# A gated mix of a long convolution and a GELU layer on one core: new front schedule, bias seeded in PSUM, output pairs read back in the loop

## The chip, the core and the metric

One core of a Trainium2 chip. TensorE (PE) multiplies, VectorE (DVE) and ScalarE (ACT) do elementwise work, GpSimd (POOL) and SyncE (SP) issue transfers here, ACT a few; DMA engines move the data between memory and the core. SBUF is the working memory, PSUM the eight banks (128 partitions of 512 fp32 each) into which TensorE writes. The metric is the time of one execution in microseconds (us), as a median over runs; less is better.

## The reference

The input x has 2048 rows (time) and 512 columns (channels). Everything is fp32.

```python
x = A_u                                             # (1, 2048, 512)
g = sigmoid((x * gate_w).sum(-1, keepdims=True))    # one gate per row
# a: per channel d a causal convolution over time with K[d, l], plus a skip term
K = einsum("dn,dnl,dn->dl", Cc, exp(dt * A * l), dt * Bc).real     # 128 complex modes n
a = irfft(rfft(pad(x)) * rfft(pad(K)))[:2048] + x * Dskip
# b: a two-layer network, 512 -> 1792 -> 512
b = gelu(x @ w1 + b1) @ w2 + b2
out = g * a + (1 - g) * b
```

## The kernel before

The kernel has three parts: a *front*, a *loop* of 16 steps and a *last stage*. The convolution is done as a transform in two stages, a product per frequency, and the inverse in two stages.

**Front** (`front`, lines 317 to 1070). Four streams of tasks share the engines:

- `dense`: the network b. Each fp32 factor is split into a rounded part and a remainder ("h" and "l"), and a product is made of three matmuls. The hidden layer has 14 columns of 128. Time is cut into 8 blocks of 256 rows, and the 8 blocks are run twice, once for each half of the hidden columns, so there are 16 passes (b = 0 to 15) of four steps each: 64 steps. A step does `hidden` (L889, matmuls L899 to L901, gelu L916, rounding L919, remainder L929) for one or two columns, and `output` (L933, matmuls L947 to L949), which adds into one of two PSUM accumulators `acc`, one for each 128 rows of the block. After the fourth step ACT scales an accumulator by 1 - g into `io` (L968) and it is stored to `out` (first half, plain, SP) or added to it in memory (second half, an accumulating transfer on POOL). In the first half, before a pass's first product, a matmul of a matrix of ones with a two-row tile (rounded b2 and its remainder) starts the accumulation with the bias (L942); `bias` (L848) prepares that tile.
- `signal`: 8 tasks, each the first transform stage of 256 rows of x. Two tiles `ux` are loaded (L417), `first_stage` (L392) makes 16 matmuls (L403) into four PSUM banks, ACT copies the four banks to tiles of a ring `st` of three (L421), and SP stores each tile in two halves to memory, `tu_d` (L424).
- `taps`: makes K. DVE and ACT build powers, magnitudes and phases for 16 groups of 32 channels, `contract` (L671) multiplies them out on PE (L681, 128 matmuls a group), and for each two groups `first_stage` runs on the result; the tables are stored to `tk_d` (L723).
- `early`: loads 27 of the 32 tiles of `tu_d` back into SBUF (L446), into places that other work has left.

The order in which the front's tasks stand on each engine is not written by hand. Each task has an engine, a modelled length and a due time; `Plan.run` (L231) walks a clock, gives every engine the earliest due task whose inputs are ready by its model, and the instructions are emitted in that order. The constants at the top set the due times: `T_0` and `T_MLP` for the dense steps, `K_0` and `T_KG` for the taps, `U_0` and `U_GAP` for the signal, `W_*` for curves laid over them, and `D_*` for offsets of single tasks (`D_EV` for the copies out of the first stage's banks and the scaling L968, `D_S1` for the first stage's matmuls, `D_XL` for the loads of x). Each queue is in order: an instruction that waits holds up all that stand behind it on its engine, SP's transfers included.

**Loop** (`conv`, L1073). For each of 16 steps: `signal(s + 1)` (8 matmuls, second stage of the signal, four banks with the tag `pu`), `taps(s + 2)` (8 matmuls, ACT copies the result, L1116), `product(s)` (six DVE operations), `inverse(s)` (8 matmuls, L1147, two banks with the tag `pa`) and `turn(s)`: ACT copies to `sa` (L1153), SP stores to `t4_d` (L1155), and after each fourth step four transfers of 512 KB bring a group back across partitions into `den` and `t3` (L1163; on POOL, for the last group on ACT). The loads of the tap tables for later steps (L1089) are on SP too. Some products of the network's last pass (`late`) run on PE at the end of the loop.

**Last stage** (L1230). Eight pairs of output tiles, m = 0 to 7: eight matmuls (L1236) into two banks; for m < 6 DVE scales one bank by g and ACT the other (L1248, L1250), and POOL adds the pair to `out` in memory with an accumulating store (L1255). Pairs 6 and 7 were loaded from `out` in loop steps 12 and 13 (L1220); DVE does their scaled add (L1246) and plain stores follow (L1252, L1257).

Of the kernel before, what the change touches and what calls it, by code (L numbers as in the profile page):

```python
# [17 lines left out]
P = 128  # L18
# [15 lines left out]
T_0 = 22.7  # L34
T_MLP = 411.78
K_0 = 24.88
T_KG = 373.15
U_0 = -15.83
U_GAP = 12.75
LAG = 12.23  # L40
TABLE = 9.03
D_KA = -63.09
D_KP = 0.01
D_S1 = 19.39
D_EV = -65.14
D_H = -60.13
D_LO = -10.68
PS = (2, 3, 1, 2)
N_ACC, N_H, N_PK, N_PU = PS
D_SP = 2.63  # L50
MEM = (6, 2, 3)
N_LD, N_HL, N_ST = MEM
D_XS = -33.08
D_G = 1.83
N_WARM = 13
T_EARLY, T_LOFT, T_DEN = 376.87, 422.84, 432.0
Y_K, Y_U = 41.11, 36.03
W_MLP = (-0.0634, -0.0326, 0.0273)
W_KG = (-0.0624, -0.0351, -0.0316)
W_U = (-0.058, -0.1265, 0.0001)  # L60
D_MAG = 0.58
D_ROT = 1.16
D_CON = 0.62
D_PHA = 0.72
D_PRE = 0.04
D_XL = -26.72
D_COE = 0.25
D_OUT = -5.37
N_LATE = 2
N_REST = 3  # L70
N_KEEP = 4

# [131 lines left out]
class Plan:  # L204
# [5 lines left out]
    def add(self, part, hold, fn, due, reads=(), writes=(), table=None, done=None, after=(), rows=1.0):  # L210
# [9 lines left out]
        t.rows = rows  # L220
# [10 lines left out]
    def run(self):  # L231
        clock = Clock()
        free = dict.fromkeys(("PE", "ACT", "DVE", "POOL", "SP", "GP"), 0.0)
# [4 lines left out]
        table, order, dma = None, [], 0.0  # L238
        for _ in self.tasks:
# [13 lines left out]
            hold = clock.run(at, t.hold, t.rows) if p == "PE" else t.hold  # L253
# [5 lines left out]
            if p in ("SP", "GP"):  # L259
                dma = max(dma, at + 1.2) + t.done  # L260
                end = dma + 0.9
# [13 lines left out]
def gated_mix(  # L275
# [41 lines left out]
    def front(pool, psum, keep, attic, loft, den):  # L317
# [10 lines left out]
        def act(n, fn, due, reads=(), writes=(), table=None, ops=1):  # L328

            return pl.add("ACT", 0.1 * ops + n / 1200.0, fn, due, reads, writes, table)  # L330

        def mm(hold, fn, due, reads=(), writes=(), rows=1.0):

            return pl.add("PE", hold, fn, due, reads, writes, rows=rows)

        def move(kb, fn, due, reads=(), writes=(), queue="SP", after=()):

            hold = 0.45 if queue == "SP" else 1.0
            return pl.add(queue, hold, fn, due, reads, writes, done=kb / 360.0, after=after)
# [20 lines left out]
        st, ld = rooms[1 : 1 + N_ST], rooms[1 + N_ST : 1 + N_ST + N_LD]  # L360
        gwb = rooms[1 + N_ST + N_LD]
# [16 lines left out]
        b2r = pool.tile([P, D], F32R, name="b2r")  # L378
        ones = pool.tile([P, P], F32R, name="ones")
# [12 lines left out]
        def first_stage(xs, due, evac, ahead=2):  # L392
# [12 lines left out]
            mm(1.2, products, due + D_S1, [*(key for _, key in xs), "c1"], [key for _, key in banks], 0.5)  # L405
# [5 lines left out]
        def signal():  # L411
            for s in range(8):
# [6 lines left out]
                def evac(r, pp, key, s=s, t=t):  # L419
                    k = take("st", N_ST)  # L420
                    act(512, lambda: nc.scalar.copy(st[k], pp), t + D_EV, [key], [("st", k)])  # L421
# [9 lines left out]
        def early():  # L431

            us = places(attic, loft, den)
            keys = [("ux", 0)] + [("st", k) for k in range(N_ST)]
# [17 lines left out]
        def make_dt():  # L452
# [25 lines left out]
            act(4, lambda: nc.scalar.activation(r, r, AF.Exp, scale=0.25), -200, [], ["dt"], table="exp")  # L478
# [26 lines left out]
        def prepare(u, t, eb_k):  # L505
# [25 lines left out]
            act(7 * UW, scaled, act_due, ["pr"], ["xt"], ops=7)  # L531
# [6 lines left out]
            act(11 * UW, exps, act_due, ["pr"], [("ea", u % 2), kx], "exp", ops=11)  # L538
# [17 lines left out]
            act(18 * UW, sines, act_due, [], ["xt", "xv"], "sin", ops=3)  # L556
# [45 lines left out]
        def waves(t):  # L602
            def sines():
                nc.scalar.activation(tt[:, 0], ph, AF.Abs)
                nc.scalar.activation(tt[:, 1], ph, AF.Sin, scale=TWO_PI / TURN)
                nc.scalar.activation(tt[:, 0], tt[:, 0], AF.Sin, bias=half_pi, scale=-TWO_PI / TURN)

            act(99 * CW, sines, t + D_KA, ["ph"], ["tt"], "sin", ops=3)

        def begin(c, k, t):  # L610
# [3 lines left out]
                8 * CW, lambda: nc.scalar.copy(xc[k][:, :, 0:4], x4[:, :, :, cs]), t + D_KA,  # L614
# [56 lines left out]
        def contract(u, c, k, t):  # L671
# [18 lines left out]
            for g0 in (0, 4):  # L690
                mm(1.89, lambda g0=g0: products(g0), t + D_KP, ["y0", "y1", ("xc", k)], [("pk", q)])
# [8 lines left out]
            act(512, lambda: nc.scalar.copy(xs, pks[q].rearrange("p s g -> p (s g)")), t + D_S1, [("pk", q)], [key])  # L700
# [4 lines left out]
            def evac(r, pp, key):  # L705
                act(
                    512,
# [68 lines left out]
        def split(h, lo, src, hk, lk, key, due, on_vector=False):  # L776
            if on_vector:
                vec(512, lambda: nc.vector.tensor_copy(h, src), due, [key], [hk], fast=2)
            else:
                act(512, lambda: nc.scalar.copy(h, src), due, [key], [hk])  # L780
# [51 lines left out]
        def gates(b0, b1_, t):  # L832
# [3 lines left out]
                16, lambda: nc.scalar.activation(gate[:, 0, ts], gs[:, ts], AF.Sigmoid), t,  # L836
# [11 lines left out]
        def bias():  # L848

            k, q = take("ld", N_LD), take("ld", N_LD)  # L850
            one, b2f, keys = ld[k][:, 0:P], ld[q], [("ld", k), ("ld", q)]

            def fill():
                nc.gpsimd.memset(b2f, 0.0)
                nc.gpsimd.memset(one, 0.0)
                nc.gpsimd.memset(one[0:1], 1.0)
                nc.gpsimd.memset(one[32:33], 1.0)

            def rows():
                nc.sync.dma_start(b2f[0:1], b2)  # L860
                nc.sync.dma_start(b2f[32:33], b2)

            def go():
                nc.scalar.copy(ones, one)
                nc.scalar.copy(b2r, b2f)

            def low():
                nc.vector.tensor_sub(b2r[32:33], b2f[32:33], b2r[32:33].bitcast(F32))

            pl.add("POOL", 0.5, fill, -99, [], keys)  # L870
            pl.add("SP", 0.9, rows, -98.5, [], keys, done=0.1)
            act(640, go, 0, keys, ["b2"], ops=2)
            vec(512, low, 0, keys, ["b2"])
# [15 lines left out]
        def hidden(i, t):  # L889
# [24 lines left out]
            def gelu():  # L914
# [8 lines left out]
            act(  # L923
                2 * nf * SB, gelu, t + D_H, ["b1"], [hk, ("h", q)], "gelu",
                ops=nf + 2,
            )
# [6 lines left out]
        def output(i, t):  # L933
# [4 lines left out]
            def products(s, a):  # L938
                ss = slice(s * P, (s + 1) * P)
                start = j == 0  # L940
                if start and b < NSB:
                    nc.tensor.matmul(a, ones, b2r, start=True, stop=False)  # L942
                    start = False
                for n, f in enumerate(fs):
                    w = f % FH
                    h, l = hi[:, n, ss], lo[:, n, ss]
                    nc.tensor.matmul(a, h, wh[1][w], start=start, stop=False)  # L947
                    nc.tensor.matmul(a, h, wl[1][w], start=False, stop=False)  # L948
                    nc.tensor.matmul(a, l, wh[1][w], start=False, stop=(j == 3))  # L949
# [3 lines left out]
            for s in range(2):  # L953
                if b == NB - 1 and s >= 2 - N_LATE:
# [4 lines left out]
                n = 3 * len(fs) + (1 if j == 0 and b < NSB else 0)  # L959
                mm(  # L960
                    0.2295 * n, lambda s=s, q=q: products(s, acc[q]), t + LAG + D_OUT * (j == 3),
                    [hk, lk, "b2", *ws], [("acc", q)],
                )
                if j == 3:
# [3 lines left out]
                        560, lambda n=n, q=q, r=r: nc.scalar.mul(io[r], acc[q], gate[:, 1, n : n + 1]),  # L968
                        t + D_EV, [("acc", q), ("gate", b % NSB)], [("io", r)],
                    )  # L970
                    if b < NSB:
# [4 lines left out]
                    else:  # L976
                        move(
                            256,
# [4 lines left out]
        def dense():  # L983
# [354 lines left out]
```

## Time and profile before

| | us |
|---|---|
| median of 3 runs (lowest to highest) | 539.93 (539.12 to 541.77) |
| span of the profiled execution | 539.9 |
| PE busy | 511.7 |
| DVE busy | 426.8 |
| ACT busy | 353.5 |
| POOL busy | 40.9 |
| front / loop / last stage / transfers alone after it | 424.6 / 88.0 / 17.0 / 10.3 |

The profile is one execution as the hardware recorded it. A group is all instructions of one line that write and read tiles of the same names, with the busy time, the mean length of one, the idle time of the engine just before them, and what ended that idle time. L916 stands for line 916 of the kernel before. Matmuls overlap, so the time from one start to the next is the price of one, not its own length. "PEclk" is the clock that TensorE was granted, as a part of full speed. A transfer's time to landing counts from its issue.

### The profile page before, as it was taken

What the parts mean: (1) busy time and instruction counts of PE and PEld (TensorE: products, weight loads), DVE (VectorE), ACT (ScalarE), POOL (GpSimd) and SP (SyncE); (2) the same over time, 40 slices, a digit from 0 to 9 for tenths busy, and PEclk for the clock granted to TensorE, in tenths of its full rate; (3) what the DMA queues carried; (4) which work ended last, traced back from release to release, by engine and by line L of the source; (5) the groups of instructions that cost most, each with busy time, mean ns of one, the idle gap of its engine ahead of it and who ended that gap; (6) DMA issues with size and microseconds to landing.
All of it is one profiled execution on the core that took longest, in us unless ns stands there. A gap on an engine that the chain in (4) does not pass through costs nothing.

```text
span 539.9 us, 12181 instructions
## 1 busy us (share of the span) xinstructions
PE 511.7 (95%) x4818; PEld 385.6 (71%) x4818; DVE 426.8 (79%) x806; ACT 353.5 (65%) x614; POOL 40.9 (8%) x79
## 2 busy tenths in 40 slices
PE   7878899999999999989999999999999999999981
PEld 7546789898899889777988989889888522223620
DVE  5898799999999959869999899999511388887132
ACT  4989846699875599976577987387253555555030
POOL 2000000000000000000102010101010001011040
PEclk9879999999999999999999999999999999999996
DMA  7989564162584442583887037514778758998888
GB/s 245 357 288 313 181 235 139 59 197 82 130 232 179 158 127 72 178 280 74 212 196 205 19 88 162 126 60 104 231 188 198 210 207 289 392 386 290 319 163 189
DMA packets 80837, 104.73 MB, mean 194 GB/s; under 512 B 39222, under 2 KB 43450, under 8 KB 80268
## 3 DMA queue, kind: packets, MB, share of 16 engines
q1 hardware_dynamic: 73756, 79.80, 46.7%
q0 software_dynamic: 6688, 21.79, 16.5%
q10 hardware_dynamic: 336, 2.36, 1.2%
q8 instruction: 38, 0.62, 0.4%
q14 instruction: 19, 0.16, 0.1%
HBM read 58.31 MB, written 45.62 MB: 192 GB/s over the span
## 4 chain that ended last, share of the span: by engine, by line
PE 76%; DMA 9%; ACT 8%; DVE 3%; issue 1%; SPq 1%; ACTq 0%; DVEq 0%
PE pk L681 10%; PE ph L899 8%; PE acc L947 8%; PE ph L901 8%; PE ph L900 8%; PE acc L949 7%; PE acc L948 7%; PE p2u L1108 5%; PE p2k L1108 5%; PE pa L1147 3%; PE pb L1236 3%; DMA tu_d<-attic 3%; DMA attic<-in_xs_dram 2%; PE ph L403 2%; ACT L916 1%
## 5 line engine op out<-in xcount | busy, mean ns | idle before, releaser
L899 PE MATMUL ph<-xh,wh 128*128 128x256 f32 x448 | 128.9, 288 | 3.4 <-ACT attic L421 2.2
L901 PE MATMUL ph<-xh,wl 128*128 128x256 f32 x448 | 127.6, 285 | 0.8 <-DVE wl L782 0.7
L900 PE MATMUL ph<-xlo,wh 128*128 128x256 f32 x448 | 127.2, 284 | 0.0
L899 PEld LDWEIGHTS ph<-xh,wh 128*128 128x128 f32 x448 | 85.8, 192 | 14.1 <-issue 5.6
L947 PE MATMUL acc<-wh,hh 128*128 128x512 f32 x210 | 85.1, 405 | 3.2 <-ACT hh L919 3.2
L900 PEld LDWEIGHTS ph<-xlo,wh 128*128 128x128 f32 x448 | 85.9, 192 | 2.0
L901 PEld LDWEIGHTS ph<-xh,wl 128*128 128x128 f32 x448 | 85.8, 191 | 1.6 <-DVE wl L782 1.6
L949 PE MATMUL acc<-wh,hl 128*128 128x512 f32 x210 | 83.2, 396 | 0.4 <-DVE hl L929 0.4
L948 PE MATMUL acc<-wl,hh 128*128 128x512 f32 x210 | 83.1, 396 | 0.0
L916 ACT ACTIVATE ph<-ph,b1t 128x256 f32<-128x256 f32 x112 | 50.4, 450 | 42.8 <-PE ph L901 40.8
L929 DVE TENSOR_TENSOR hl<-ph,hh 128x512 fp32r<-128x512 f32 (+1 forms) x62 | 38.5, 621 | 32.4 <-ACT hh L919 32.3
L681 PE MATMUL pk<-y,den 128*32 128x64 f32 x2048 | 61.4, 290 | 0.0
L681 PEld LDWEIGHTS pk<-y,den 128*32 128x32 f32 x2048 | 57.2, 136 | 3.7 <-issue 1.4
L947 PEld LDWEIGHTS acc<-wh,hh 128*128 128x128 f32 x210 | 39.7, 189 | 18.2 <-issue 6.8
L949 PEld LDWEIGHTS acc<-wh,hl 128*128 128x128 f32 x210 | 39.8, 190 | 11.0 <-DVE hl L929 2.1
L643 DVE TENSOR_TENSOR y<-y,ea 128x64 f32<-128x64 f32 (+4 forms) x80 | 45.5, 569 | 0.2
L948 PEld LDWEIGHTS acc<-wl,hh 128*128 128x128 f32 x210 | 39.8, 189 | 6.7
L919 ACT CAST hh<-ph 128x512 fp32r<-128x512 f32 (+1 forms) x62 | 33.0, 533 | 10.3 <-PE acc L948 6.9
L488 DVE TENSOR_TENSOR loft<-den,zz 128x256 f32<-128x256 f32 (+2 forms) x48 | 37.4, 779 | 2.7 <-ACT den L614 2.3
L489 DVE TENSOR_TENSOR loft<-den,zz 128x256 f32<-128x256 f32 (+2 forms) x48 | 37.3, 777 | 0.0
L656 DVE TENSOR_TENSOR y<-y,loft 128x2048 f32<-128x2048 f32 x16 | 36.6, 2288 | 0.0
L1116 ACT COPY k<-p2k 128x512 f32<-128x512 f32 x32 | 18.8, 586 | 25.0 <-issue 13.1
(178 smaller groups left out, 876.3 us busy)
## 6 DMA issues: line engine op xcount, KB each, us to landing
tu_d<-attic SPq DMA_DIRECT2D x64, 128.0 KB, 3.4
tk_d<-sk SPq DMA_DIRECT2D x32, 256.0 KB, 4.9
tk<-tk_d SPq DMA_DIRECT2D x32, 256.0 KB, 4.4
t_d<-sa SPq DMA_DIRECT2D x32, 256.0 KB, 4.8
t<-t_d POOLq DMA_DIRECT2D x9, 512.0 KB, 7.1
attic<-in_xt_dram SPq DMA_DIRECT2D x16, 256.0 KB, 3.8
xh_d<-xh SPq DMA_DIRECT2D x8, 512.0 KB, 3.4
xl_d<-xlo SPq DMA_DIRECT2D x8, 512.0 KB, 4.6
```

Of the source, the lines that this page charges most:

```text
L488: vec(2 * m, lambda: vv.tensor_mul(t, a, br), due, [ka, *kb], [kt])
L643: nc.vector.tensor_mul(both(n, 64 - 3 * n, n), both(0, 64 - n, n), an)
L681: nc.tensor.matmul(pks[q][32 * j : 32 * j + 32, :, gg], x[:, r, :, ch], y[:, r, :, ch], start=(r == 0), stop=(r == 1), skip_group_check=True,)
L899: nc.tensor.matmul(p, h, xh[xk][:, d], start=(d == 0), stop=False)
L900: nc.tensor.matmul(p, h, xlo[xk][:, d], start=False, stop=False)
L901: nc.tensor.matmul(p, lo, xh[xk][:, d], start=False, stop=(d == 3))
L916: nc.scalar.activation(phs[q][:, n], phs[q][:, n], AF.Gelu_apprx_tanh, bias=b1t[:, f : f + 1])
L929: nc.vector.tensor_sub(lo, phs[q][:, 0:nf], hi.bitcast(F32))
L947: nc.tensor.matmul(a, h, wh[1][w], start=start, stop=False)
L948: nc.tensor.matmul(a, h, wl[1][w], start=False, stop=False)
L949: nc.tensor.matmul(a, l, wh[1][w], start=False, stop=(j == 3))
L1108: nc.tensor.matmul(out[64 * i : 64 * i + 64], w, x, start=True, stop=True)
```

## The change

It has four parts.

1. The front's constants are new, and the planner's model with them: lengths of ACT tasks are given one by one, a change between whole-array and tiled matmuls costs 0.1 us, a queue has eight transfers under way at most, and transfers are a little slower. The signal's due times move from U_0 = -15.83 to 18.93 (the dense steps' from 22.7 to 26.15, the taps' end from 398 to 381). The ring `st` has five tiles instead of three, and each bank of the signal's first stage is stored by one transfer of 256 KB instead of two of 128 KB.
2. The bias is no longer a matmul. b2 is loaded once, repeated over all partitions (`b2a`), and ACT copies it into each accumulator before a pass of the first half (`seed`); no product of those passes starts an accumulation. The warm-up matmuls write the accumulators' banks.
3. In the loop and the last stage each PSUM bank has a name of its own instead of a place in a ring.
4. All eight output pairs are loaded back in the loop, one in each of steps 7 to 14, behind that step's stores on SP. In the last stage DVE does all sixteen scaled adds and all stores are plain, on SP (the very last on ACT).

The diff, cut:

```diff
-T_0 = 22.7
-T_MLP = 411.78
-K_0 = 24.88
-T_KG = 373.15
-U_0 = -15.83
-U_GAP = 12.75
+T_0 = 26.15
+T_MLP = 410.84
+K_0 = 33.15
+T_KG = 348.06
+U_0 = 18.93
+U_GAP = 10.84
...
-D_S1 = 19.39
-D_EV = -65.14
+D_S1 = -63.1
+D_EV = -9.88
...
-MEM = (6, 2, 3)
+MEM = (6, 2, 5)
 N_LD, N_HL, N_ST = MEM
...
+DOTS_AT = (2, 6, 7, 8, 12, 18, 21, 23)
-N_WARM = 13
+N_WARM = 12
...
-W_U = (-0.058, -0.1265, 0.0001)
+W_U = (-0.064, -0.1028, 0.0122)
...
-D_XL = -26.72
+D_XL = -98.24
...
+D_B2 = -98.57
...
                 def evac(r, pp, key, s=s, t=t):
                     k = take("st", N_ST)
-                    act(512, lambda: nc.scalar.copy(st[k], pp), t + D_EV, [key], [("st", k)])
-                    for m in range(2):
-                        move(
-                            128, lambda m=m: nc.sync.dma_start(rows[:, 8 * s + 4 * m + r], st[k][64 * m : 64 * m + 64]),
-                            t, [("st", k)], [("u_d", 8 * s + 4 * m + r)],
-                        )
+                    act(0.48, lambda: nc.scalar.copy(st[k], pp), t + D_EV, [key], [("st", k)])
+                    at = rows[:, 8 * s + r : 8 * s + r + 5 : 4].rearrange("k m d -> m k d")
+                    move(
+                        256, lambda: nc.sync.dma_start(at, st[k]), t,
+                        [("st", k)], [("u_d", 8 * s + 4 * m + r) for m in range(2)],
+                    )
...
-        def bias():
...
+        def seed(q, due):
+
+            act(0.52, lambda: nc.scalar.copy(acc[q], b2a), due, ["b2a"], [("acc", q)])
...
-                start = j == 0
-                if start and b < NSB:
-                    nc.tensor.matmul(a, ones, b2r, start=True, stop=False)
-                    start = False
+                seeded = b < NSB
+                start = j == 0 and not seeded
...
+                    if b + 1 < NSB:
+                        seed(q, t + D_EV)
...
-            bias()
             move(1, lambda: nc.sync.dma_start(b1t, b1), -98, [], ["b1"])
+            move(256, lambda: nc.sync.dma_start(b2a, b2.to_broadcast([P, D])), D_B2, [], ["b2a"])
...
-                pu = ps.tile([P, D], F32, tag="pu", name=f"p2u{s}{c}", bufs=4)
+                pu = ps.tile([P, D], F32, tag=f"pu{s % 2}{c}", name=f"p2u{s}{c}", bufs=1)
...
-        if 12 <= s < 14:
-            k = s - 6
+        if 7 <= s < 15:
+            k = s - 7
             room(k)
             nc.sync.dma_start(mos[k], out[2 * k : 2 * k + 2].rearrange("s p d -> p s d"))
...
-            if m < 6:
-                room(m)
-            for i in range(2):
                 t = 2 * m + i
-                z, g = mos[m][:, i], gate[:, 0, t : t + 1]
-                if m > 5:
-                    nc.vector.scalar_tensor_tensor(z, pbs[i], g, z, ALU.mult, ALU.add)
-                elif i:
-                    nc.scalar.mul(z, pbs[i], g)
-                else:
-                    nc.vector.tensor_scalar(z, pbs[i], g, None, ALU.mult)
+                z = mos[m][:, i]
+                nc.vector.scalar_tensor_tensor(z, pb, gate[:, 0, t : t + 1], z, ALU.mult, ALU.add)
                 if m == 7:
                     (nc.sync, nc.scalar)[i].dma_start(out[t], z)
-            to = out[2 * m : 2 * m + 2].rearrange("s p d -> p s d")
-            if m < 6:
-                nc.gpsimd.dma_start(to, mos[m], accum_op=ALU.add)
-            elif m < 7:
-                nc.sync.dma_start(to, mos[m])
+            if m < 7:
+                nc.sync.dma_start(out[2 * m : 2 * m + 2].rearrange("s p d -> p s d"), mos[m])
```

More of the change, by code (lines that the diff above doesn't have):

```diff
@@ L252, in run @@
             ready[p].remove(t)
-            hold = clock.run(at, t.hold, t.rows) if p == "PE" else t.hold
+            hold = t.hold
+            if p == "PE":
+                turn = SWITCH if t.tiled != tiled else 0.0
+                tiled = t.tiled
+                hold = clock.run(at, turn + hold, t.rows)
             if t.table and t.table != table:
@@ L326, in vec, with act, mm @@
             return pl.add("DVE", 0.07 + n / 960.0 / fast, fn, due, reads, writes)
[L328 to L334, printed above, removed]
+        def act(hold, fn, due, reads=(), writes=(), table=None):
+            return pl.add("ACT", hold, fn, due, reads, writes, table)
+        def mm(hold, fn, due, reads=(), writes=(), rows=1.0, tiled=False):
+            t = pl.add("PE", hold, fn, due, reads, writes, rows=rows)
+            t.tiled = tiled
+            return t
         def move(kb, fn, due, reads=(), writes=(), queue="SP", after=()):
[L338 to L339 removed]
+            hold = 0.5 if queue == "SP" else 1.0
+            return pl.add(queue, hold, fn, due, reads, writes, done=kb / 320.0, after=after)
         acc = tiles(N_ACC, [P, D], "acc", space=psum)
```

149 lines of the change are left out of this document (67 added, 82 removed).

## The prediction

> **What bounds the kernel now.** I read the busy times by stage first, then the timeline of TensorE (PE) where it is not full, then the waits, the issues of transfers and the last 40 us of the timeline. In the first view, the columns are the stretch, its length, each engine's busy time, the granted clock, the share of the DMA engines and their GB/s:
>
> ```profile
> 0.00:25.00 25.00, 20.10 (x104) 17.09 (x105) 17.98 (x37) 17.10 (x35) 3.57 (x14) 0.93 0.90 304
> 25.00:50.00 25.00, 18.75 (x119) 11.49 (x118) 21.83 (x55) 22.26 (x40) 0.00 (x0) 0.86 0.89 292
> 50.00:75.00 25.00, 23.19 (x250) 19.24 (x248) 21.94 (x56) 18.49 (x31) 0.66 (x2) 1.00 0.63 211
> 75.00:200.00 125.00, 125.00 (x1414) 108.99 (x1416) 118.82 (x223) 94.56 (x158) 2.27 (x8) 1.00 0.48 149
> 225.00:250.00 25.00, 23.44 (x265) 18.59 (x264) 20.35 (x37) 17.43 (x36) 1.18 (x3) 1.00 0.61 199
> 250.00:424.60 174.60, 174.60 (x1986) 154.17 (x1986) 134.64 (x245) 111.63 (x187) 19.76 (x33) 1.00 0.62 154
> 424.60:512.60 88.00, 87.20 (x438) 29.20 (x438) 61.49 (x100) 43.29 (x83) 6.19 (x12) 1.00 0.84 299
> 512.60:529.60 17.00, 14.43 (x64) 4.37 (x61) 7.51 (x10) 4.13 (x6) 7.13 (x6) 1.00 0.91 174
> 529.60:539.90 10.30, 0.00 (x0) 0.00 (x0) 0.00 (x0) 0.00 (x0) 0.00 (x0) 0.57 0.73 185
> ```
>
> Four regimes. From 75 us to 512 us PE is full (125.00 of 125, 174.60 of 174.60, 87.20 of 88), so work taken off PE there is worth its whole length. Before 75 us PE has holes. From 512.6 to 529.6 it has 2.6 us of them, and the last 10.3 us hold nothing but transfers. The holes before 75 us, on the timeline of PE (start, length, what; in brackets the idle time before it and who ended it):
>
> ```profile
> 29.71 1.04 PE L403 MATMUL ph<-attic,c1t 32*64 32x512 f32 x2 [1.39 <-DMA attic<-in_xl_dram]
> 32.98 1.11 PE L403 MATMUL pu<-attic,c1t 32*64 32x512 f32 x1 [0.91 <-ACT attic L421]
> 36.47 0.58 PE L899 MATMUL ph<-xh,wh 128*128 128x256 f32 x1 [1.52 <-ACT attic L421]
> 36.85 0.41 PE L900 MATMUL ph<-xlo,wh 128*128 128x256 f32 x1
> 37.06 0.41 PE L901 MATMUL ph<-xh,wl 128*128 128x256 f32 x1
> 43.48 0.64 PE L403 MATMUL pu<-attic,c1t 32*64 32x512 f32 x1 [1.48 <-ACT attic L421]
> 48.35 0.39 PE L899 MATMUL ph<-xh,wh 128*128 128x256 f32 x1 [0.73 <-ACT attic L421]
> 48.81 0.28 PE L899 MATMUL ph<-xh,wh 128*128 128x256 f32 x1
> 48.93 0.28 PE L900 MATMUL ph<-xlo,wh 128*128 128x256 f32 x1
> ```
>
> All of these are the signal's first stage (L403): PE waits for its input or for ScalarE (ACT) to empty its banks (L421), and then runs at half rate, one product per 0.21 us at 36.85 against 0.12 us at 48.81. ACT in turn waits for its stores:
>
> ```profile
> ACT attic L421 <- DMA tu_d<-attic: 12.0, 6, 6.1
> PE acc L942 <- ACT io L968: 1.8, 1, 1.8
> ```
>
> The first row: 12.0 us in 6 waits, 6.1 us the longest.
>
> **The change, part by part.** The median shown is 539.93 us and the profiled execution spans 539.9 us, so the sum is made against that.
>
> *Later signal, a ring of five store tiles instead of three, one store per bank instead of two.* Between 25 and 75 us PE idles 6.25 + 1.81 us, and the clock of 0.86 costs 0.14 x 25 = 3.5 us: 11.6 us in all. With five tiles a stage's four banks can leave PSUM without waiting for any store of that stage, and dense work stands in PE's queue where the signal now waits. I take 9 us off: the gaps are the signal's own, but its eight stages still have to run, and ACT is 89% busy there. Bounds: 12 us off, or nothing, should the same waits turn up wherever the stages now lie. Fewer issues on SyncE (SP), 32 in place of 64, cost nothing and hide nothing; SP is not on the path there.
>
> *Seeded bias.* Sixteen products with the ones matrix (L942) go; ACT copies the bias into the accumulator instead.
>
> ```profile
> 24.62 0.39 PE L949 MATMUL acc<-wh,hl 128*128 128x512 f32 x1
> 24.85 0.40 PE L947 MATMUL acc<-wh,hh 128*128 128x512 f32 x1
> L942 PE MATMUL acc<-b2r,ones 128*128 128x512 f32 x16 | 6.9, 430 | 1.8 <-ACT io L968 1.8
> L968 ACT ACTIVATE io<-acc,gate 128x512 f32<-128x512 f32 x30 | 20.2, 694 | 14.7 <-PE acc L949 13.5 <-DMA attic<-in_xl_dram 1.2
> L421 ACT COPY attic<-pu 128x512 f32<-128x512 f32 x16 | 9.5, 596 | 12.0 <-DMA tu_d<-attic 12.0
> ```
>
> A product of that size takes 0.23 us (24.62 to 24.85), so 16 x 0.23 = 3.7 us come off a full PE. The copies cost ACT 16 x 0.60 = 9.6 us (a copy of that shape, L421), of which two stand at the start. They stand behind the scaling of the finished accumulator (L968, 0.69 us): the next block's first product now waits for both, and on ACT the gelu steps queue behind them. What covers them is the dense work between a block's last product and the next block's first one: PE waited once for L968 in the whole run (1.8 us). So 0.5 us, the one place made longer; if every one of the 14 later hand-overs paid the copy, 8 us. The 256 KB load of the broadcast bias goes in among the first weights in place of two small rows: at 304 GB/s that is 0.9 us, behind which all weights queue on SP. I take 0.4 us, between 0 and 0.9.
>
> *The rest of the new order* (earlier x loads, later dot products, first stages and contractions at high priority) changes which work stands beside which, on an engine that is full: 0 us, from -5 to +5 by the 1.6 us idle at 225 to 250 us and by a few waits of the size above. The front: -9 - 3.7 + 0.5 + 0.4 = -11.8 us.
>
> *Loop.* Naming the banks leaves the rotation as it is: four for the signal, two for the inverse. Six more pairs of 512 KB are read, one per step behind that step's stores on SP, 3.1 MB in all.
>
> ```profile
> 434.29 1.02 PE pa L1147 x8
> 438.89 1.02 PE pa L1147 x8
> ```
>
> ```profile
> 470.40:475.00 4.60, 4.60 (x26) 1.27 (x24) 3.68 (x7) 2.24 (x5) 0.00 (x0) 1.00 1.06 404
> 488.80:493.40 4.60, 4.60 (x26) 1.27 (x24) 3.65 (x7) 2.25 (x5) 2.04 (x4) 1.00 0.51 111
> ```
>
> A step is 4.60 us, all PE. But at 470 us the DMA engines are full at 404 GB/s, so 3.1 MB are 7.8 us of their time; half of a step (2.3 us) is free at 489 us, and I estimate some 4 us free between there and the last stage. Queued on SP ahead of the last stores (L1155), on whose landing the last stage waits, the reads can delay it by 0 to 3.8 us; I take 1.5 us, since the loads' first buffers, at step 7, are read out long before and wait for nobody.
>
> *Last stage.* The six accumulating stores go, and every pair becomes a scaled add on VectorE (DVE) and a plain store.
>
> ```profile
> 511.62 0.64 PE L1236 MATMUL pb<-den,g1t 128*64 128x512 f32 x1
> 521.44 1.94 PE L1236 MATMUL pb<-t,g1t 128*64 128x512 f32 x8 [0.85 <-DVE loft L1250]
> 524.23 4.51 PE L1236 MATMUL pb<-t,g1t 128*64 128x512 f32 x20 [0.85 <-DVE loft L1250]
> 527.93 1.61 DVE L1246 SCALAR_TENSOR_TENSOR attic<-pb,gate,attic 128x512 f32<-128x512 f32 x2
> ```
>
> ```profile
> out_dram<-attic POOLq DMA_DIRECT2D x3, 512.0 KB, 7.9
> out_dram<-attic SPq DMA_DIRECT2D x1, 256.0 KB, 8.9
> xh_d<-xh SPq DMA_DIRECT2D x8, 512.0 KB, 3.4
> ```
>
> PE does 64 products at 4.51/20 = 0.226 us, 14.4 us, if no bank is late; DVE needs 16 x 0.80 = 12.9 us beside it (two in 1.61 us), so it keeps up and ends about 1.0 us later: 511.6 + 14.4 + 1.0 = 527.0 instead of 529.5. The last store on SP was issued at 528.7 and took 8.9 us behind the accumulating ones, to 537.6; the execution ended 2.3 us after that. Without them I take the 3.4 us of an undisturbed 512 KB store: 527.1 + 3.4 + 2.3 = 532.8. That is -7.1 us, and -5.6 with the 1.5 us of the loop.
>
> Sum: 539.9 - 11.8 - 5.6 = 522.5; I forecast 522 us, with a range of its own of 508 to 532.
>
> **The rivals.** *A: the joined stores are slow, and the kernel gets slower.* The new store writes one tile of 128 rows to an address pattern whose outermost dimension is 2 (`m k d`), where the old one wrote 64 rows at a time with 64 outermost. Should such a store run on two of the sixteen DMA engines, each at 404/16 = 25 GB/s, its 256 KB take 5.2 us and a stage's four 21 us, and everything else on SP has a share queued behind them on those two. The first four stages are due 6.8, 12.3 and 22 us apart (from U_0, U_GAP and W_U), so the ring lacks 14 + 9 us, less one store for its fifth tile: 18 us in which ACT stands at L421 with every gelu behind it and PE runs dry, plus some 4 us for the x loads behind them. 522 + 22 = 544, from 532 to 560. For: the trace has ACT waiting 12.0 us for these stores even now. Against: no store of this trace has that pattern, and the later signal leaves slack between later stages. It decides as soon as a store takes over 5 us to land in a row of four. The Trainium skill ("DMA: Bandwidth & Descriptors", section "Why a DMA increments its semaphore by 16 and not by 1") states just this: a transfer uses the largest number of engines up to 16 that divides the slowest dimension of both its sides, which here would be two. No run here shows it yet; by that rule the sum would be 544 and not 522.
>
> *B: the taps become last.* When PE gains 12 us, the loop cannot start before the taps are back from memory.
>
> ```profile
> 386.82 3.77 PE pk L681 x127
> 426.34 1.08 PE p2k L1108 x4
> ```
>
> ```profile
> 401.00 10.16 SPq L723 DMA_DIRECT2D tk_d<-sk  x8
> 414.59 1.75 SPq L1089 DMA_DIRECT2D tk<-tk_d  x4
> ```
>
> The last contraction ended at 390.6, the stores ran until 411.2 and the reads began at 414.6. With the taps no earlier than now, the loop can start at some 419 us instead of 414.5: 527 us. For: DVE, which makes them, is 95% busy from 75 to 200 us. Against: the taps' due times end 17 us earlier (K_0 + T_KG 381 for 398) and DVE is at 77% from 250 us on.
>
> *C: the loop pays for the reads.* All 7.8 us return as delay of the last stage, 6.3 more than I take: 528 us. The Trainium skill ("DMA: Bandwidth & Descriptors", section "Specifications") gives a limit of about 358 GB/s per core for HBM; the 404 GB/s above do not agree with it, and by it the reads would be 8.8 us.
>
> **How the numbers follow.** A change within 0.5% (2.7 us) cannot be told from none. The forecast has 0.49, A 0.20, B 0.13, C 0.12, and 0.06 stay for the gains and losses cancelling. Faster by over 0.5%, below 537.2: 0.49 + 0.13 + 0.12 + 0.03 = 0.77. Within: 0.05. Slower, above 542.6: 0.18, nearly all of it A. The low end, 508, is the forecast with all 11.6 us recovered (-2.6), the loop free (-1.5), 2.5 us less in landing and 5 us from the order, with 3 for what I have not seen in the first 25 us. The high end, 541, takes in B and C and the lower part of A, and leaves about 0.16 above it.
>
> **What would show it.** Right: between 25 and 75 us PE busy above 46 of 50 us and the clock at 1.00; no L942; the front ending near 413 us; steps of 4.60 us; the last store landing in 4 us. A shows as landings of 7 us and more for the stores to tu_d and waits of ACT for them; B as a gap of PE before the first tap product; C as a last stage that starts over 90 us after the loop did. The forecast is wrong if ACT's copy of the bias shows as PE's releaser at many blocks.

## The result, and the profile after

The changed kernel takes 579.88 us (median of 4 runs, 578.06 to 580.43), the kernel before 540.38 us beside it: a ratio of 1.0707, with a 95% interval of 1.0679 to 1.0735. It is 39 us slower where 18 us faster was forecast, and lies outside the range. What happened is rival A, at over twice the price that the prediction gave it. Ratios, here and below, leave out runs over 1.5% slower than the fastest of the same kernel, which is one run of the kernel with its stores on GpSimd's queue.

The stages by the starts of their first matmuls on PE, in the profiled executions (the third column is the first kernel of the experiments):

| us | before | after | split |
|---|---|---|---|
| start to the loop's first tap product | 424.5 | 464.7 | 406.1 |
| from there to the last stage's first product | 87.2 | 93.3 | 91.2 |
| from there to the end | 28.3 | 19.9 | 20.1 |
| span | 539.9 | 577.9 | 517.4 |

The loss lies in the front, 40.2 us; the loop is 6.1 us longer, and what follows it gives 8.4 back. The stretches of the changed kernel, with the columns of the prediction's first view:

```profile
25.00:50.00 25.00, 22.49 (x143) 18.90 (x142) 21.94 (x57) 23.34 (x48) 0.53 (x1) 0.93 0.85 299
50.00:75.00 25.00, 18.61 (x126) 16.13 (x124) 16.84 (x32) 17.80 (x30) 0.00 (x0) 0.89 0.42 140
75.00:200.00 125.00, 103.89 (x1114) 85.11 (x1118) 91.10 (x185) 85.72 (x140) 1.04 (x5) 0.88 0.43 135
250.00:300.00 50.00, 33.20 (x331) 26.72 (x330) 32.00 (x66) 30.95 (x51) 1.19 (x3) 0.86 0.56 160
300.00:464.70 164.70, 164.17 (x1913) 145.71 (x1911) 132.77 (x243) 109.55 (x180) 18.68 (x31) 1.00 0.54 137
464.70:558.00 93.30, 88.52 (x434) 31.62 (x435) 61.00 (x100) 42.81 (x81) 6.17 (x12) 1.00 0.90 325
558.00:574.30 16.30, 15.51 (x64) 5.34 (x64) 12.01 (x16) 0.00 (x0) 0.00 (x0) 0.90 0.71 275
574.30:577.90 3.60, 0.00 (x0) 0.00 (x0) 0.01 (x1) 0.00 (x0) 0.00 (x0) 1.00 0.55 208
```

Where PE was full before, it now stands: 21 us of the 125 from 75 us on, 17 of the 50 from 250 us on, and a clock of 0.86 to 0.89 on top. No other engine is full there either, and the DMA engines move less than before (from 75 to 200 us 135 GB/s in place of 149). The last two rows, in contrast, are what the change was to give: 3.6 us of transfers alone at the end in place of 10.3. Three short stretches, in the same columns, show what the DMA engines do meanwhile:

```profile
55.00:60.00 5.00, 5.00 (x37) 3.74 (x22) 4.90 (x10) 4.43 (x6) 0.00 (x0) 1.00 0.13 51
80.00:85.00 5.00, 5.00 (x47) 3.85 (x49) 2.37 (x4) 0.59 (x1) 0.00 (x0) 0.67 0.13 51
95.00:100.00 5.00, 0.00 (x0) 0.00 (x0) 2.17 (x5) 4.91 (x7) 0.00 (x0) 0.70 0.13 51
```

The page of the profile has no landing times for SP's transfers in this profile, so the sign that the prediction gave for A, landings of 7 us and more, can't be read from it; these rows stand in for it. A DMA share of 0.13 is that of two engines out of sixteen, and the rate does not move from 51 GB/s, 25.5 for each; a tile of 262,144 bytes takes 5.1 us at that. The timeline of ACT, whose copies empty the first stage's banks into the ring, is paced by it:

```profile
61.85 0.59 ACT L433 COPY attic<-pu 128x512 f32<-128x512 f32 x1 [2.39 <-DMA tu_d<-attic]
66.94 0.58 ACT L433 COPY attic<-pu 128x512 f32<-128x512 f32 x1 [4.50 <-DMA tu_d<-attic]
87.38 0.58 ACT L433 COPY attic<-pu 128x512 f32<-128x512 f32 x1 [4.54 <-DMA tu_d<-attic]
92.51 0.59 ACT L433 COPY attic<-pu 128x512 f32<-128x512 f32 x1 [4.54 <-DMA tu_d<-attic]
```

61.85 to 66.94 and 87.38 to 92.51: one copy per 5.1 us. The Trainium skill ("DMA: Bandwidth & Descriptors", section "Why a DMA increments its semaphore by 16 and not by 1") gives two engines for an outermost dimension of two; the trace agrees, with 0.13 and 51 GB/s. And the transfers of SP's queue, by its own timeline (start, time in which SP stands in the issues, line, count):

```profile
58.72 4.93 SPq L828 DMA_DIRECT2D xh_d<-xh  x1
63.74 0.48 SPq L828 DMA_DIRECT2D xl_d<-xlo  x1
64.27 3.29 SPq L785 DMA_DIRECT2D attic<-in_xs_dram  x2
72.03 12.03 SPq L436 DMA_DIRECT2D tu_d<-attic  x3
84.15 5.50 SPq L959 DMA_DIRECT2D out_dram<-io  x2
```

An issue can be a matter of 0.48 us (63.74). Behind joined stores it can take as long as a store does: 4.93 us for one rounded block of x, 12.03 for three stores, 5.50 for two outputs. The Trainium skill ("Perfetto Trace Analysis", section "DMA Instruction — HWDGE (DVE, Sync)") lets such a row begin when the waits for semaphores are over and end when the descriptors are made and the issuing engine is free for its next instruction; the trace agrees in so far as its list of waits holds none of these times. So loads that have nothing to do with the signal's stores come late, and the list of waits names them beside ACT's own:

```profile
ACT s L712 <- DVE pk L709: 21.3, 6, 12.4
DVE attic L838 <- DMA attic<-in_xs_dram: 16.1, 4, 9.9
ACT attic L433 <- DMA tu_d<-attic: 16.0, 4, 4.5
DVE pr L530 <- DMA pr<-in_prm_dram: 11.7, 2, 11.5
```

ACT's wait for its own stores, all that rival A priced at its ring, is 16.0 us here (18.6 with another row of 2.6 for the tiles named `st`). DVE stands 16.1 us for x and 11.7 us for the taps' parameters. The first row is further down the same line: ACT waits for DVE's results in the taps, 21.3 us, where it was 5.9 before.

### The profile page after: what moved, and what is told of

Read it like the earlier page. It is cut to its first block, busy times and chain, and to the rows that moved or that the text cites. A ratio compares the mean times of both kernels' runs of the same rounds, so it can differ in the third digit from the quotient of the medians.

```text
span 577.9 us, 12134 instructions
## 1 busy us (share of the span) xinstructions
PE 518.0 (90%) x4800; PEld 392.5 (68%) x4800; DVE 432.1 (75%) x812; ACT 366.6 (63%) x630; POOL 32.8 (6%) x69
## 4 chain that ended last, share of the span: by engine, by line
PE 53%; DMA 25%; ACT 12%; DVE 6%; issue 2%; SPq 2%; ACTq 0%; DVEq 0%
PE pk L693 7%; DMA tu_d<-attic 6%; PE acc L931 6%; PE acc L932 5%; PE acc L933 5%; PE ph L888 5%; PE ph L889 5%; PE ph L890 5%; PE p2k L1097 4%; PE p2u L1097 4%; DMA attic<-in_xs_dram 3%; DMA pr<-in_prm_dram 3%; DMA tk<-tk_d 3%; PE pb L1225 3%; PE ph L415 2%; PE pa L1136 2%
## 5 line engine op out<-in xcount | busy, mean ns | idle before, releaser
L931 PE MATMUL acc<-wh,hh 128*128 128x512 f32 x210 | 88.9, 423 | 9.4 <-ACT hh L908 6.8
L888 PEld LDWEIGHTS ph<-xh,wh 128*128 128x128 f32 x448 | 86.7, 194 | 14.7 <-DVE hl L915 8.4
L932 PE MATMUL acc<-wl,hh 128*128 128x512 f32 x210 | 85.2, 406 | 0.0
L933 PE MATMUL acc<-wh,hl 128*128 128x512 f32 x210 | 84.8, 404 | 0.0
L931 PEld LDWEIGHTS acc<-wh,hh 128*128 128x128 f32 x210 | 41.4, 197 | 34.0 <-issue 13.2
L933 PEld LDWEIGHTS acc<-wh,hl 128*128 128x128 f32 x210 | 41.2, 196 | 9.7 <-DVE hl L915 0.2
L932 PEld LDWEIGHTS acc<-wl,hh 128*128 128x128 f32 x210 | 41.5, 198 | 6.8
```

The source lines that it names most:

```text
L888: nc.tensor.matmul(p, h, xh[xk][:, d], start=(d == 0), stop=False)
L931: nc.tensor.matmul(a, h, wh[1][w], start=start, stop=False, skip_group_check=seeded)
L932: nc.tensor.matmul(a, h, wl[1][w], start=False, stop=False, skip_group_check=seeded)
L933: nc.tensor.matmul(a, l, wh[1][w], start=False, stop=(j == 3), skip_group_check=seeded)
```

## The experiments

Each kernel was timed beside the kernel before. "Split" is the changed kernel with its store as two DMAs of 64 rows.

**Split.**

```diff
-at = rows[:, 8 * s + r : 8 * s + r + 5 : 4].rearrange("k m d -> m k d")
-move(256, lambda: nc.sync.dma_start(at, st[k]), t, ...)
+for m in range(2):      # in one move of 256 KB, same place in the order
+    nc.sync.dma_start(rows[:, 8 * s + 4 * m + r], st[k][64 * m : 64 * m + 64])
```

> The changed kernel with each store of the signal's first stage issued as two of 64 rows again; the order on TensorE, VectorE and ScalarE is unchanged. Theory 1 (the joined store runs on two of sixteen DMA engines, 256 KB at 51 GB/s take 5.1 us, and ScalarE stands behind it): the front gets back to 414 to 424 us (it ended at 464.7), the total is 520 to 535, and no stretch of the first 200 us shows a DMA share of 0.13 for long. Theory 2 (the new order itself starves TensorE: dense steps behind first stages of high priority, whose banks are emptied late): the total stays above 560, and the same instructions wait for one another with the stores landing fast.

519.73 us (519.15 to 520.77), ratio 0.9620 (0.9594 to 0.9646), just below the first theory's 520 to 535; the front ends at 406.1 us, earlier than its 414 to 424. PE, DVE and ACT have the same instructions in the same order as in the changed kernel, so the 60 us between the two are the form of the store alone. The same kernel was timed again for the later groups.

> The split kernel once more, as the measure for the other kernels of this group on the same chip. Both theories: a ratio of 0.960 to 0.965 to the kernel before.

519.38 us, ratio 0.9586 (0.9554 to 0.9617). Its stretches:

```profile
25.00:50.00 25.00, 23.07 (x154) 19.99 (x153) 23.15 (x61) 24.66 (x50) 0.53 (x1) 1.00 0.88 305
50.00:75.00 25.00, 25.00 (x281) 20.98 (x280) 24.09 (x47) 24.64 (x39) 0.12 (x1) 1.00 0.87 292
75.00:200.00 125.00, 124.24 (x1452) 107.00 (x1452) 122.35 (x239) 108.40 (x179) 2.36 (x9) 1.00 0.51 158
```

PE holds 48.1 of the 50 us from 25 to 75 at full clock; the prediction asked for over 46. No wait of ACT for a store of the signal is left, and none of DVE for x or the parameters; ACT's wait for the taps is 6.4 us. PE's own waits add up to 11 us, against 55 in the changed kernel, so about 44 of the 60 us are idle time of PE; the rest fits the lower granted clock, a mean of 0.950 there and 0.995 here.

**The joined store alone, on the kernel before.**

```diff
-nc.sync.dma_start(rows[:, 8 * s + 4 * m + r], st[k][64 * m : 64 * m + 64])   # m = 0, 1
+nc.sync.dma_start(at, st[k])                                                # once, at m = 0
```

> The kernel before with the joined store alone, its order on all three engines unchanged. Theory 1: 8 stages x 4 stores x 5.1 us = 164 us on two engines behind a ring of only three tiles, so ScalarE waits at least as long as in the changed kernel; total 565 to 600. Theory 2: the store costs little in an order that was made for early stages; 540 to 550.

609.19 us, ratio 1.1267 (1.1242 to 1.1292), above the 565 to 600 expected: 68 us from one line. The wait of ACT that was 12.0 us in 6 times:

```profile
ACT attic L421 <- DMA tu_d<-attic: 56.8, 13, 7.7
```

The new order is not to blame: the old one, with its ring of three, loses 68 us to the same store where the new one loses 60.

**Two halves by columns.** Each joined store as two DMAs of 128 rows by 256 columns (`at[:, :, c]`, `st[k][:, c]`), the outermost dimension still 2.

> The changed kernel with each joined store issued as two DMAs of 128 rows by 256 columns, each still with the two blocks as its outermost dimension: twice as many DMAs of half the size. If the outermost dimension of 2 sets the engines that a store uses, each half runs on two engines too, 128 KB in some 2.6 us, a store takes 5.1 us as before, and the time stays at 575 to 600 us. If it was the size of one store, or the number of stores in flight, the halves land like those of the split kernel and the time is 518 to 528 us.

585.92 us, ratio 1.0823 (1.0779 to 1.0867). Half the size and twice the number change nothing for the better:

```profile
80.00:85.00 5.00, 5.00 (x48) 3.88 (x50) 2.46 (x4) 0.68 (x2) 0.00 (x0) 0.71 0.14 48
```

The same two engines. Splitting by rows helped because it changed the outermost dimension, not because it made two transfers of one. A whole tile as one transfer with another outermost dimension was not run.

**One and two joined stores of each four**, the others split.

> The split kernel with one store of each four joined (the first), and the other three as two DMAs of 64 rows. If each joined store has its price, a quarter of 60 us comes back: 532 to 538 us. If the price only comes up where several joined stores fill the two engines one behind the other, 8 stores of 5.1 us spread over some 190 us cost next to nothing: 519 to 524 us.

> The split kernel with the first two stores of each four joined. If the price comes up only where stores fill the two engines one behind the other, two of 5.1 us are hidden behind three other buffers and the others' evictions: 520 to 528 us. If the price goes with the number beyond the first, a third of 58 us for each further one: 535 to 545 us.

521.56 us (0.9627, 0.9592 to 0.9662) and 529.51 us (0.9759, 0.9696 to 0.9822). At the split kernel's two ratios, a mean of 0.960, one joined store in four is 1 us, two are 8, and four were 60. A joined store has no fixed price: eight of 5.1 us in the front's 400 find room. The three points fit a price that starts where a stage's joined stores (10 us for two, 20.5 for four) reach or exceed the 9.6 and 12.5 us from one start to the next of the first three stages in the split kernel (43.5, 53.1 and 65.6 us). With two joined, PE loses its time where those stages lie:

```profile
50.00:75.00 25.00, 21.59 (x183) 16.93 (x185) 19.77 (x38) 17.39 (x30) 0.00 (x0) 0.93 0.61 188
75.00:100.00 25.00, 21.57 (x238) 19.02 (x234) 18.30 (x35) 20.40 (x30) 0.12 (x1) 0.93 0.53 179
```

The second expectation gave 520 to 528 to this reading, and it came out a little above.

**The stores on ScalarE's queue.** `nc.scalar.dma_start(at, st[k])`.

> The changed kernel with its joined stores issued from ScalarE's queue in place of SyncE's; nothing else is moved. A store still has two engines and some 5.1 us. If most of the loss beyond the prediction's 22 us comes from SyncE's other transfers (inputs, weights, parameters), which stand behind the stores in one queue: 535 to 560 us, with 16 us of it at most for 32 issues of 0.5 us on ScalarE. If the stores' own duration holds ScalarE's evictions, and with them TensorE, whatever queue they are in: 570 to 590 us.

608.19 us, ratio 1.1223 (1.1175 to 1.1271), outside both expectations. Two rows of ACT's timeline show why:

```profile
91.10 8.24 ACTq L436 DMA_DIRECT2D tu_d<-st  x1
99.44 0.59 ACT L433 COPY attic<-pu 128x512 f32<-128x512 f32 x1 [7.75 <-DMA attic<-in_xt_dram]
```

The issue itself stands for 8.24 us, and with it ACT, which has the gelu steps to do; the bracket puts the idle time down to a load of x that landed meanwhile, but the row above it covers the time. The expectation had put 0.5 us on an issue. The engine that issues pays for the slow transfers ahead in its queue.

**The stores on GpSimd's queue**, where little else stands. `nc.gpsimd.dma_start(at, st[k])`.

> The changed kernel with its joined stores issued from GpSimd's queue in place of SyncE's; GpSimd is busy some 2.6 us in the first 100. If what cost 60 us is that the issue stands on an engine that has other transfers or work to give out, most of it goes, and what is left is what the evictions wait for their own stores, 22 us by rival A: 530 to 550 us. If the stores' own duration holds the evictions and these cost it all, 570 to 590 us. If this queue spreads the store over more engines, the share of the DMA engines is above 0.13 while only stores run, and the time is 518 to 530 us.

532.08 us (526.55 to 535.42), ratio 0.9786 (0.9704 to 0.9868), in the range of the first expectation. This tells less than it seems to, since two things changed: the engine that issues, and the rate at which the stores go. Two copies of ACT's timeline:

```profile
63.41 0.59 ACT L433 COPY attic<-pu 128x512 f32<-128x512 f32 x1 [1.97 <-DMA tu_d<-attic]
65.84 0.58 ACT L433 COPY attic<-pu 128x512 f32<-128x512 f32 x1 [1.84 <-DMA tu_d<-attic]
```

The copies follow each other by 2.4 us and not 5.1, though a single store lands 9.4 to 20.1 us after its issue: several are under way at once, together at 108 GB/s (262,144 bytes in 2.43 us), which two engines at 25 GB/s would not give. And the issue stands only 0.80 us, on POOL:

```profile
L436 POOL DMA_DIRECT2D tu_d<-attic x20: 796/798/839, 46.7 to 255.6; - x20
...
DMA to landing us min/median/max: 9.4/13.9/20.1
```

**The loads that stand behind the stores moved instead.** The stores stay on SP and on two engines; x, weights and parameters that are loaded after the first store are issued from GpSimd, in the changed kernel and, as a measure of the move itself, in the split one.

> The changed kernel with its joined stores on SyncE as they are, and the inputs, weights and parameters that are loaded after the first store issued from GpSimd's queue. If the loads behind the stores make most of the 60 us, what is left is ScalarE's wait for its own stores, 18.6 us in the trace of the changed kernel: 535 to 548 us, plus what the move costs by itself (the next kernel). If the evictions carry it, 565 us and more.

> The split kernel with the same loads issued from GpSimd's queue. Both readings: the price of the move itself, which the kernel beside it has to be read with; by the landing times of 256 KB on that queue (5.2 us for the accumulating stores) the loads come some 2 us later, 519 to 526 us.

553.22 us (1.0184, 1.0127 to 1.0240) and 521.13 us (0.9597, 0.9553 to 0.9641). The move costs nothing by itself, and takes 28 of the changed kernel's 60 us away (at 542 us, 1.0707 less 1.0184). What stays is 32 us (553.2 less 521.1), and ACT's waits for stores in this kernel are as long:

```profile
ACT attic L437 <- DMA tu_d<-attic: 23.4, 5, 8.3
ACT io L956 <- DMA out_dram<-io: 7.0, 1, 7.0
ACT st L437 <- DMA tu_d<-st: 3.0, 1, 3.0
```

23.4 + 7.0 + 3.0 = 33.4 us; the 7.0 are for outputs whose stores stand behind the joined ones. By this the loss is near half and half: ACT for its stores, and everyone for loads behind them. The first half is a reading and not shown: PE's waits are only 26 us longer here than in the split kernel with the same move (38.6 for 12.5), the rest fits its lower clock (0.961 for 0.997), and no run took ACT's waits away alone. The expectation of 535 to 548 took 18.6 us for the first half, from a kernel in which waits for loads stood in front of some of ACT's.

**The other parts of the change, on the split kernel.** The old signal times (three lines of the kernel put into one here):

```diff
-U_0, U_GAP, W_U = 18.93, 10.84, (-0.064, -0.1028, 0.0122)
+U_0, U_GAP, W_U = -15.83, 12.75, (-0.058, -0.1265, 0.0001)
```

> The split kernel with the signal's start, spacing and warp as they were before the change (start -15.83, spacing 12.75, warp -0.058, -0.1265, 0.0001); the ring of five, the seeded bias and all else stay, and the planner orders the front anew. If the later signal brought what the prediction says (most of 9 us, from the stretch of 25 to 75 us), it goes: 525 to 530 us. If the ring, the bias and the rest of the order bring the gain without it, within 2 us of the split kernel: 518 to 522 us.

547.33 us, ratio 1.0105 (1.0065 to 1.0144), far above both expectations.

```profile
25.00:50.00 25.00, 13.81 (x82) 9.56 (x82) 24.15 (x61) 22.79 (x41) 0.56 (x1) 0.79 0.88 291
50.00:75.00 25.00, 22.21 (x137) 18.62 (x137) 22.27 (x44) 18.52 (x31) 0.00 (x0) 0.87 0.67 225
```

18 of the 28 us are lost in the stretch that the prediction named (13.81 x 0.79 + 22.21 x 0.87 = 30.2 us at full clock, for 48.1), so the later signal does clear it. But it is less there than the 39.3 us of the kernel before, which had the same signal times: the planner's other offsets are set for the later one, so this run gives the place and not the size. A ring of three (`MEM = (6, 2, 3)`; the order is planned anew):

> The split kernel with three buffers for the stores of u's transform in place of five; the planner's other parameters are kept, and it orders the front anew for three. If the ring of five brought most of the 9 us that the prediction gave to the two together, 525 to 530 us; if the later signal alone did it, within 2 us of the split kernel, 518 to 522 us.

522.02 us, ratio 0.9650 (0.9611 to 0.9690): 1 to 4 us of the gain can be the ring's, not most of it. The bias as 16 matmuls again, without ACT's 16 copies (two copies and a subtraction prepare the bias's tile):

> The split kernel (519.7 us) with the bias of the first eight blocks added by TensorE again, 16 matmuls of 0.23 us, and ScalarE's 16 copies of 0.5 us left out; the order of everything else is kept. If TensorE bounds the front, as the prediction's 3.7 us has it: 523.4 us (522.4 to 524.4). If ScalarE's copies cost what the matmuls gave (its place on the path): no change or a gain, 517 to 520 us.

521.54 us, ratio 0.9628 (0.9591 to 0.9665), 0.4 to 2.3 us above the two split runs by the ratios, with intervals of 1.5 to 2 us each way. 3.7 us are at the edge of what this allows, and none is not excluded. The kernel before's loop and last stage behind the split front, and the changed kernel's behind the front of before:

> As split, with the loop and the last stage of the kernel before. In the changed kernel the loop was 8.0 us longer (from the first tap product to the first product of the last stage, 93.3 for 85.3) and what follows 8.4 us shorter (19.9 for 28.3). Theory 1 with rival C of the prediction (the reads come back in full as delay of the last stage): within 2 us of split. The sum on record (the new end is worth 5.6 us): 5 to 6 us slower than split. If the long loop came from taps that arrived late because of the slow stores, the new end is worth 7 us and more here.

> The kernel before with the loop and last stage of the changed one, front untouched. Rival C: 538 to 541. The sum on record: 533 to 536. In both the loop's steps stay at 4.60 us, and the last store lands within 4 us of its issue.

523.38 us (0.9675, 0.9641 to 0.9709) and 535.50 us (0.9920, 0.9888 to 0.9952): by the medians the new end is worth 3.7 us on the one and, at 541.0 us for the kernel before beside it, 5.5 on the other; by the ratios 3 and 4.3. In the profiles, loop and what follows take 114.7 us with the old end behind the split front and 110.6 to 111.3 with the new one; behind the front of before they take 115.4 and 112.4. So 3.1 to 4.1 us are the end's own. Last, the loads of pairs 5 to 7 behind the last loads of the inverse's data, and the additions of the network's late sums put off to the last pair:

```diff
+if k < 5:
     nc.sync.dma_start(mos[k], ...)
+# behind turn(15):
+for k in (5, 6, 7): nc.scalar.dma_start(mos[k], ...)
```

> The split kernel with the output pairs 5 to 7 loaded behind the last loads of the inverse's data in place of steps 12 to 14, and the two additions of the late sums put ahead of the last pair. If those 1.5 MB ahead of the last stores are what lengthens the way from the last inverse to the last stage (14.6 us against 10.9 us before the change), this returns most of it: 516 to 518 us. If the transfers only move behind into a last stage that waits for them, or the lengthening has another cause: 519 to 522 us.

520.16 us, ratio 0.9601 (0.9566 to 0.9636): nothing. From the last inverse to the last stage it is 11.9 us in place of 14.7, and from there to the end 22.4 in place of 20.1. The transfers moved behind into a stage that then waited for them (DVE 2.2 and 1.5 us).

None of these kernels is faster than the split one, 519.4 to 519.7 us, which is faster than both kernels of the case.

## Why the prediction was wrong

**The step that failed** is the sentence on the stores: "Fewer issues on SyncE (SP), 32 in place of 64, cost nothing and hide nothing; SP is not on the path there." By the issues of that line in the changed kernel (count, then shortest, median and longest in ns):

```profile
L436 SPq DMA_DIRECT2D tu_d<-attic x20: 483/2734/7332, 48.5 to 304.1; - x20
L436 SPq DMA_DIRECT2D tu_d<-st x12: 488/2230/5239, 53.9 to 297.9; - x12
```

SP stood 86 us in these 32 issues (the sum over them) against 45 us in the 64 of before and 42 in the 64 of the split kernel; the term that the sum put at nothing measured 60 us. Before, the median of them was 0.59 us:

```profile
L424 SPq DMA_DIRECT2D tu_d<-attic x64: 445/588/5339, 28.3 to 269.1; - x64
```

The number of issues says little; how long each stands went with how fast the transfers ahead of it did.

**Rival A's mechanism was right**, and its durations to the number: 5.2 us for a store against 5.1, 21 us for four against 20.5, ACT standing at the copies. Two things about it were wrong. Its price was 22 us: 18 for the ring in the first three gaps and 4 for the loads of x. Measured against the split kernel it is 60. Of these, 28 went when the loads behind the stores were moved to another queue, and the 32 that stayed are as long as ACT's waits for stores. The sum let only the loads of x wait, though it had said itself that "everything else on SP has a share queued behind them", and it stopped after the third gap, while PE lost 17 of 50 us at 250 us too. And its chance was 0.20. What spoke against it, that "no store of this trace has that pattern", was a lack of rows and no evidence. The rule of the Trainium skill that the prediction cites for A fitted the edit exactly, with nothing in the trace against it, and that deserved more than one in five.

**The rest of the sum came out close, in part by luck.** It gave 522.5 us, a ratio of 0.968; with the store split it is 0.959 to 0.962. But the front gained 6 us more than its terms, and the loop cost 2 to 3 us more than its own. By the terms, from the profiled executions:

- Front: -18 us (424.5 to 406.1 or, in the second run, 406.5) for -11.8. The stretch of 25 to 75 us, as busy time by clock: 23.07 + 25.00 = 48.1 after, 18.75 x 0.86 + 23.19 = 39.3 before, 8.8 us for the 9 taken. The first 25 us, put at nothing, gave 21.49 x 1.00 against 20.10 x 0.93, 2.8 us (2.2 in the first run, with 20.85), of which the clock's part can differ from run to run (it is 0.93 there in the changed kernel). The bias gave between 0 and 3.7. That makes 11 to 15 us; the other 3 to 7 were not traced to a part of the order.
- Hand-overs with the copied bias: 0.5 us taken, 0.5 in the changed kernel and 0.3 in the split one, whose row for the first product of an output step ends with ACT's copy (L865):

```profile
L934 PE MATMUL acc<-wh,hh 128*128 128x512 f32 x210 | 85.4, 407 | 1.0 <-ACT io L955 0.7 <-ACT acc L865 0.3
```

- Loop: a step stays at 4.60 us (the tap products of four steps start at 418.34, 422.95, 427.55 and 432.15 us in the split kernel); the whole is 3.4 to 4.1 us longer for 1.5, at the top of its bound of 3.8. Rival C had all 7.8 return; about half did, and the two kernels with an end exchanged show that the end as a whole still gains. That the reads cause this half is only partly shown: with three of them moved, the way from the last inverse to the last stage got 2.8 us shorter. Last stage: 28.3 us down to 20.1, 8.2 us for 7.1.
- Rival B did not come: in the split kernel the last tap contraction ends at 379.7 us, 11 us earlier than before, and the loop starts 26 us behind it. A trace of its sign is there all the same: PE waits 0.9 us in the one run and 1.4 in the other for the first table of the taps. B's own sum had a slip. It counts from 426.3 us, where a later product starts (414.5 after the gain); the first one starts at 424.5, which gives 412.7 and so some 529 us for 527. The expectation for the old end has the same start in its 85.3 us for the loop.

```profile
406.10 1.20 PE L1100 MATMUL p2k<-tk,cc 128*64 128x512 f32 x3 [0.89 <-DMA tk<-tk_d]
```

## What to carry to other kernels

Before two DMAs are joined into one, look at the outermost dimension that the joined pattern has: the number of transfers is worth 0.5 us of the issuing engine each, the number of engines that a transfer uses was worth 60 us here. A slow transfer is priced by its whole queue, not by its own consumer: list what is issued behind it on that engine and who waits for each, over all stages of the kernel, and ask how its length compares with the distance of its repeats. And when one line of a large change matches a rule exactly, run the change without that line first.

## What the runs showed of the hardware

- A DMA of 128 rows of 2 KB with an outermost dimension of 2 went at 51 GB/s on two engines from SyncE's queue, at 48 to 51 in halves of 1 KB rows; the split kernel's halves, 128 KB with 64 rows outermost, landed in 3.3 us at the median.
- Behind such stores an issue stands, up to 7.3 us on SyncE and 10.3 us on ScalarE, and what is behind it on that engine starts later. That the queue was full is a reading; no row shows how full it was. The waits of the profile do not show it; the length of the issue in the queue's timeline does.
- GpSimd's queue took one joined store after the other at 2.4 us, with a single one landing in 13.9 us at the median; how it divides them among the engines was not measured.
- A step of the split kernel's loop ran at the rate of the busiest one before, 406 GB/s for 404, with six more pairs to read:

```profile
474.00:478.60 4.60, 4.60 (x28) 1.05 (x27) 3.68 (x7) 2.25 (x4) 1.55 (x4) 1.00 1.05 406
```
